# Retention and an MLP in one kernel: the attention work of two chunks joined into larger TensorE groups

## The chip, the cores and the metric

The kernel runs on one core of a Trainium2 chip. The metric is the device time of one execution in microseconds (us). Of the kernel before, five executions took 311.14 to 312.42 us, median 312.0.

A core has five engines that run side by side and meet through semaphores: TensorE (PE: matmuls, with weight loads that overlap them, PEld), VectorE (DVE), ScalarE (ACT), GpSimd (POOL) and SyncE (SP, which here issues DMAs). Each engine takes its instructions in the order in which the code issues them. Matmul results land in PSUM, which has eight banks of 128 x 512 float32; TensorE can only reuse a bank when the engine that empties it is done. TensorE and VectorE or ScalarE work on SBUF otherwise.

## The reference

Inputs are q, k and v (8 batches, 8 heads, 576 positions, 64 dimensions) and two weights (512 x 2048 and 2048 x 512). Per batch and head:

```python
scores = scale * q @ k.T                       # 576 x 576
Dmat   = where(i >= j, gamma_h ** (i - j), 0)  # gamma_h = 1 - 2 ** (-5 - h)
attn   = (scores * Dmat) @ v                   # 576 x 64
```

The heads' results stand side by side as rows of x (4608 x 512), and the output is

```python
h = x @ w_in
g = 0.5 * h * (1 + tanh(c * (h + 0.044715 * h ** 3)))
out = g @ w_out
```

## The kernel before, in words

**Attention in chunks.** The 576 positions of a batch are four chunks of 128 and a tail of 64. The powers of gamma are multiplied into k and q when they are cast to float16 (`cast`, L232), so that within a chunk only a causal mask is left. The steps of a chunk c of batch b are:

- `turn` (L275): TensorE transposes k and q of the chunk (batches 0 to 2 and all tails). From batch 3 on `turn_dma` (L293) does it for a whole batch with two DMA transposes on SP's queue, which wait for the batch's casts.
- `score` (L304): eight matmuls per chunk, of 64 rows each, in pairs that use the upper and lower half of the array (64x128); two PSUM banks. VectorE multiplies each bank by the mask and writes it as float16 into a `ret` tile (L319).
- `state` (L328) and `scan` (L341): eight matmuls of k against v, with 64 columns each (128x64), give the chunk's part of the running state; VectorE adds it to the state so far and decays it (`vs`, `ws`).
- `spread` (L351): ScalarE casts the two halves of the state into a block-diagonal float16 tile (`tbd`; after the last chunk `tbt`, which the tail uses).
- `av` (L356): eight matmuls of `ret` against v (128x64), then, for c > 0, four full matmuls (128x128, L381) that add the product with the state of the chunks before. The tail adds four of 64 columns (L373).
- `put` (L389): ScalarE copies the result out of PSUM into `xT`, the transposed input of the MLP.

A tail holds two groups of four heads one above the other, so it is half as wide. It is loaded, cast and processed some stages after its batch.

**MLP in stages.** Stage t (0 to 8) computes 512 rows: t < 8 the four chunks of batch t, stage 8 all tails. Stages 1 to 8 have 30 steps. Steps 0 to 15 are `up` (L403): four matmuls of 128 x 512 into one of two `hp` banks, and ScalarE's GELU into `gT`; 128 of the inner 2048 per step. Stage 1 uses `up_half` (L419) in these steps. After every fourth step VectorE forms sums and differences of the blocks of `gT` (`act_sums`, L473, four instructions). Steps 16 to 29 are `prod` (L485): seven block products (a Strassen-like scheme with weight sums made once, `weight_sums`, L461), each in two steps of eight matmuls of 256 columns into bank A, B or C, in the order 1, 6, 5, 7, 2, 3, 4. `after` (L505) combines them on VectorE and ScalarE: after product 1 ScalarE copies A, after product 6 (step 19) VectorE adds B (L531), and product 7 (steps 22, 23) goes on adding into the same bank B.

**The order.** All engines' order is written by hand. `at(t, u, f)` (L629) hangs work behind step u of stage t, and works hung on one step run in the order in which they were registered. The sums of a step come after all that hangs on it. Batch b = t + 1 is processed in stage t. `group` (L666) issues one chunk per group: its scores, its state, then the values (`av`) of the group before; `put` a step later and the two spreads two and three steps later. In stages 2 to 6 the groups stand behind steps 6, 11, 16, 21 (chunks 0 to 3) and 26 (the tail of batch t - 2); in stage 1 behind 8, 13, 18 and 23, in stage 7 (the last three tails) behind 2, 7 and 12. Banks of the attention work are t0, t1 and t2 in turn for scores and states, and C or `hp` for values.

From batch 3 on, the casts of batch t + 2 hang on stage t, steps 16 to 23. GpSimd casts k and q, ScalarE v. GpSimd first runs a one-element copy, `gate` (L704), that waits for the last sum of step 15, and loads are held (`q_ld["hold"]`) until `turn_dma` behind step 24 has issued the transposes. Tails are loaded from GpSimd's queue (six DMAs each, L83).

## Time and profile before

| what | value |
|---|---|
| median of 5 executions | 312.0 us |
| the profiled execution | 311.83 us, its span 309.9 us |
| mean granted TensorE clock | 0.996 of full |
| TensorE busy | 297.8 us, 96% of the span |
| VectorE, ScalarE, GpSimd busy | 181.0, 170.3, 121.6 us |
| stage 1 | starts at 55.54, ends at 91.77 us |
| stage 2 | ends at 123.98 us |
| stages 3 to 6 | 31.41 us each, the last ends at 249.63 us |
| stage 7 | ends at 278.82 us |
| the last matmul | starts its row at 304.69, ends at 305.7 us |

The profile comes from one execution. The span runs from its first to its last instruction; what lies outside the span (1.9 us) is the same program's start and end. Lists of instructions give start and length in us, the engine, the line of the kernel, the operation, and the tiles written and read. A matmul's start is recorded, its end is modelled and lies after the start of the next, so distances between starts say more about TensorE than lengths. A list of waits gives who waited for whom, the total, the number and the longest.

### The profile page before, as it was taken

To read this page: it belongs to the slowest core of one execution; us is meant where nothing else is said; L and a number is where in the kernel's file an instruction comes from. 1 tells how busy PE (TensorE), PEld (TensorE's weight loads), DVE (VectorE), ACT (ScalarE), POOL (GpSimd) and SP (SyncE) were. 2 spreads that over 40 slices of the span, in tenths; PEclk is the share of its full clock that TensorE was granted. 3 is DMA by queue.
4 is the path that set the end of the run, shared out by engine and by line. 5 is a ranking of instruction groups with operands and counts; after the bars stand their busy time and mean duration, and the time that the engine had idled before them with its cause. 6 is when DMAs were issued, how large, how long until landed. Compare 5 with 4: busy or idle time off the path is not lost.

```text
span 309.9 us, 6884 instructions
## 1 busy us (share of the span) xinstructions
PE 297.8 (96%) x2779; PEld 199.2 (64%) x2779; DVE 181.0 (58%) x368; ACT 170.3 (55%) x327; POOL 121.6 (39%) x177
## 2 busy tenths in 40 slices
PE   7889999899998999999999999999999999999994
PEld 3458755688884488448844785478547854784583
DVE  6651766789954676476637673776376545522431
ACT  6566417877545763576357745664466346406600
POOL 8669114650871069105910591049651430000000
PEclk9999999999999999999999999999999999999998
DMA  7999999999999995997499849933920040003004
GB/s 204 216 316 376 361 271 225 220 238 244 206 173 183 218 269 116 207 204 221 86 212 212 222 75 180 223 118 69 271 73 19 17 172 0 2 0 135 2 0 135
DMA packets 125983, 51.82 MB, mean 167 GB/s; under 512 B 114176, under 2 KB 116736, under 8 KB 125952
## 3 DMA queue, kind: packets, MB, share of 16 engines
q1 hardware_dynamic: 123936, 47.72, 71.5%
q0 software_dynamic: 1536, 3.15, 4.5%
q10 hardware_dynamic: 480, 0.52, 0.6%
q8 instruction: 21, 0.34, 0.5%
q14 instruction: 10, 0.08, 0.1%
HBM read 36.70 MB, written 9.44 MB: 149 GB/s over the span
## 4 chain that ended last, share of the span: by engine, by line
PE 77%; DMA 6%; SPq 5%; POOL 4%; issue 3%; DVE 2%; ACT 2%; POOLq 0%; DVEq 0%
PE hp L409 30%; PE opB L498 12%; PE opA L498 8%; PE opC L498 8%; PE hp L426 5%; PE op L445 4%; SPq L95 3%; PE st L313 3%; DMA tt<-cq 3%; PE xs L363 2%; DMA ld<-in_moe_w_in_dram 2%; POOL cq L253 2%; PE xs L381 2%; PE us L333 2%; DMA ld<-in_q_dram 2%
## 5 line engine op out<-in xcount | busy, mean ns | idle before, releaser
L409 PE MATMUL hp<-xT,w_in_sb 128*128 128x512 f16 x448 | 101.4, 379 | 0.0
L415 ACT ACTIVATE gT<-hp 128x512 f16<-128x512 f32 x112 | 66.8, 597 | 51.2 <-PE hp L409 50.6
L409 PEld LDWEIGHTS <-w_in_sb 128*128 128x128 f16 x448 | 42.6, 98 | 49.1 <-issue 2.9
L319 DVE TENSOR_TENSOR ret<-st,cm 128x512 f16<-128x512 f32 x64 | 41.1, 684 | 23.6 <-PE st L313 23.5
L498 PEld LDWEIGHTS <-gT 128*128 128x128 f16 x512 | 49.2, 98 | 7.6 <-issue 0.7
L253 POOL TENSOR_TENSOR ck<-ld,sc 128x512 f16<-128x512 f32 x31 | 34.6, 1115 | 22.0 <-DMA ld<-in_k_dram 20.5
L498 PEld LDWEIGHTS <-s 128*128 128x128 f16 x384 | 37.2, 98 | 4.2
L480 DVE TENSOR_TENSOR s<-gT 128x512 f16<-128x512 f16 x32 | 13.6, 426 | 40.8 <-ACT gT L415 39.9
L498 PE MATMUL opA<-w_out_sb,gT 128*128 128x256 f16 x256 | 32.4, 273 | 0.0
L426 PE MATMUL hp<-xT,w_in_sb 128*128 128x256 f16 x256 | 30.1, 273 | 2.3 <-POOL w_in_sb L565 1.0
L498 PE MATMUL opB<-wt,gT 128*128 128x256 f16 x256 | 30.7, 273 | 0.5 <-DVE ost L512 0.5
L426 PEld LDWEIGHTS <-w_in_sb 128*128 128x128 f16 x256 | 24.5, 98 | 6.0 <-issue 1.8
L704 POOL COPY gate<-s 128x1 f16<-128x1 f16 x5 | 0.9, 187 | 68.7 <-DVE s L483 68.7
L253 POOL TENSOR_TENSOR cq<-ld,sc 128x512 f16<-128x512 f32 x24 | 26.1, 1089 | 2.7 <-DMA ld<-in_q_dram 2.7
L399 ACT CAST xT<-xs 128x512 f16<-128x512 f32 x32 | 18.7, 586 | 12.4 <-PE xs L381 11.8
L432 ACT ACTIVATE gT<-hp 128x512 f16<-128x512 f32 x32 | 19.1, 597 | 8.4 <-PE hp L426 8.4
L354 ACT CAST tbd<-ws 64x256 f16<-64x256 f32 x48 | 19.4, 403 | 5.7 <-DVE ws L349 5.1
L240 ACT CAST cv<-ld 128x512 f16<-128x512 f32 x27 | 16.2, 619 | 2.8 <-DMA ld<-in_v_dram 2.5
L512 DVE TENSOR_TENSOR k<-k,opB 128x512 f32<-128x512 f32 x16 | 10.9, 684 | 10.2 <-PE opB L498 10.1
L512 DVE TENSOR_TENSOR ost<-k,opC 128x512 f32<-128x512 f32 x16 | 11.0, 687 | 9.6 <-PE opC L498 9.4
L565 DVE CAST w_out_sb<-ld 128x512 f16<-128x512 f32 x16 | 9.1, 582 | 12.3 <-DMA ld<-in_moe_w_out_dram 12.3
L498 PE MATMUL opC<-w_out_sb,s 128*128 128x256 f16 x128 | 16.1, 273 | 0.0
(97 smaller groups left out, 381.3 us busy)
## 6 DMA issues: line engine op xcount, KB each, us to landing
ld<-in_q_dram SPq DMA_DIRECT2D x32, 256.0 KB, 5.2
ld<-in_k_dram SPq DMA_DIRECT2D x32, 256.0 KB, 5.4
ld<-in_v_dram SPq DMA_DIRECT2D x32, 256.0 KB, 5.1
out_dram<-ost SPq DMA_DIRECT2D x16, 512.0 KB, 4.7
ld<-in_moe_w_in_dram SPq DMA_DIRECT2D x16, 256.0 KB, 5.8
ld<-in_moe_w_out_dram SPq DMA_DIRECT2D x16, 256.0 KB, 6.1
lt<-in_k_dram POOLq DMA_DIRECT2D x16, 64.0 KB, 4.6
lt<-in_q_dram POOLq DMA_DIRECT2D x16, 64.0 KB, 4.5
```

The source lines that it names most:

```text
L240: eng.copy(out=dst, in_=raw)
L253: eng.tensor_tensor(out=dst.rearrange("p (h d) -> p h d", d=D), in0=raw.rearrange("p (h d) -> p h d", d=D), in1=sc[:, s0 : s0 + nh].unsque ...
L319: nc.vector.tensor_tensor(out=r[:, 0:w], in0=st[hl][:, 0:w], in1=m.rearrange("p n i -> p (n i)"), op=ALU.mult)
L354: cp(out=(tbd[b % 2][r, c, :, r] if c < NC - 1 else tbt[b % 4][r, :, r]), in_=att[b]["w"][r])
L399: nc.scalar.copy(out=xT[:, g0 : g0 + 2], in_=src)
L409: nc.tensor.matmul(hp.rearrange("p (g t) -> p g t", t=TL), w_in_sb[:, ct, 128 * fc : 128 * fc + 128], xT[:, o : o + TB // TL, ct, :], star ...
L415: nc.scalar.activation(out=gT[t][:, fc].rearrange("p i n -> p (i n)"), in_=hp, func=AF.Gelu_apprx_tanh)
L426: nc.tensor.matmul(hp[:, 256 * x : 256 * x + 256].rearrange("p (g t) -> p g t", t=TL), w_in_sb[:, ct, 128 * (f + x) : 128 * (f + x) + 128] ...
L432: nc.scalar.activation(out=gT[t][:, f : f + 2, 2 * u : 2 * u + 2, :].rearrange("p f i n -> p f (i n)"), in_=hp.rearrange("p (f n) -> p f n ...
L480: nc.vector.tensor_tensor(out=s["1"], in0=a21, in1=a22, op=ALU.add)
L498: nc.tensor.matmul(op[tag][:, HD * u : HD * u + HD], lhs(f), rhs[:, f], start=(new and u == 0 and f == 0), stop=(f == NH - 1), skip_group_ ...
L512: nc.vector.tensor_tensor(out=o, in0=a, in1=b, op=ALU.add)
```

## The change

From batch 2 on, the attention work is issued in larger groups. In stage t, for batch b = t + 1 and, from stage 3 on, the tail of batch e = t - 3:

- behind step u0: the scores of chunks 0 and 1 and of the tail;
- behind u1: the states of chunks 2 and 3 (both into one bank), the values of chunks 0 and 1 and of the tail, and then all their products with the states (now a function of its own, `inter`);
- behind u2: the scores of chunks 2 and 3;
- behind u3: the states of chunks 0 and 1 of the next batch, and the values and products of chunks 2 and 3.

The four steps are 11, 17, 21, 26 in stage 1, 8, 14, 19, 25 in stage 2, and 6, 12, 17, 24 in stages 3 to 6. A tail's turn moves to step 3 of its stage, its casts from step 15 to 14, and it is processed a stage later. In stage 7 tails 4 and 5, then 6 and 7 go through in pairs. Banks are named by hand: scores also use A, B, C and `hp`. The `ret` tiles become four of full width and two of half width for tails of batches 0 to 4 and 6, in place of five of full width. In stage 1 the casts and the turns of batch 2 move to other steps.

```diff
--- before.py
+++ after.py
@@ -315,9 +315,10 @@
                 )
         m = cm if c < NC else tm
         for hl in range(2):
-            r = sb.tile([128, 512], F16, tag="ret", name="ret", bufs=5)
+            tag, n = ("ret", 4) if c < NC or b in (5, 7) else ("rett", 2)
+            r = sb.tile([128, 512 if tag == "ret" else 256], F16, tag=tag, name=tag, bufs=n)[:, 0:w]
             nc.vector.tensor_tensor(
-                out=r[:, 0:w], in0=st[hl][:, 0:w], in1=m.rearrange("p n i -> p (n i)"), op=ALU.mult
+                out=r, in0=st[hl][:, 0:w], in1=m.rearrange("p n i -> p (n i)"), op=ALU.mult
             )
             a["ret"][c, hl] = r
 
@@ -325,39 +326,38 @@
         c = c % NC
         return slice(512 * c + 128 * p + 64 * hl, 512 * c + 128 * p + 64 * hl + 64)
 
-    def state(b, c, tag="att"):
-        a = att[b]
-        us = bank(tag, "us")
+    def state(b, c, us=None, n=0):
+        a = att[b]
+        us = bank("att", "us") if us is None else us
         for p in range(HP):
             for hl in range(2):
                 nc.tensor.matmul(
-                    us[64 * hl : 64 * hl + 64, 64 * p : 64 * p + 64],
+                    us[64 * hl : 64 * hl + 64, 256 * n + 64 * p : 256 * n + 64 * p + 64],
                     a["k"][:, col(c, p, hl)],
                     a["v"][:, col(c, p, hl)],
                     start=True, stop=True,
                 )
-        a["U"] = us
+        a["U", c] = us[:, 256 * n : 256 * n + 256]
 
     def scan(b, c):
         a = att[b]
-        uc = a.pop("U")[:, 0:256].rearrange("p (q d) -> p q d", d=64)
+        uc = a.pop(("U", c)).rearrange("p (q d) -> p q d", d=64)
         if c > 0:
             s = sb.tile([128, HP, 64], F32, tag="vs", name="vs", bufs=2)
             nc.vector.tensor_tensor(out=s, in0=uc, in1=a["w"], op=ALU.add)
             uc = s
-        a["w"] = w = sb.tile([128, HP, 64], F32, tag="ws", name="ws", bufs=2)
+        a["w"] = a["w", c] = w = sb.tile([128, HP, 64], F32, tag="ws", name="ws", bufs=2)
         nc.vector.tensor_tensor(out=w, in0=uc, in1=gt, op=ALU.mult)
 
     def spread(b, c, cp, hls=(0, 1)):
         for hl in hls:
             r = slice(64 * hl, 64 * hl + 64)
-            cp(out=(tbd[b % 2][r, c, :, r] if c < NC - 1 else tbt[b % 4][r, :, r]), in_=att[b]["w"][r])
+            cp(out=(tbd[b % 2][r, c, :, r] if c < NC - 1 else tbt[b % 4][r, :, r]), in_=att[b]["w", c][r])
 
     def av(b, c, tag="att"):
         a = att[b]
         n = HP if c < NC else 2
-        td = tbd[b % 2]
-        xs = bank(tag, "xs")
+        a["xs", c] = xs = bank(tag, "xs")
         for p in range(n):
             for hl in range(2):
                 nc.tensor.matmul(
@@ -366,6 +366,9 @@
                     a["ret"][c, hl][:, 128 * p : 128 * p + 128],
                     start=(p == 0), stop=True, skip_group_check=True,
                 )
+
+    def inter(b, c):
+        xs = att[b]["xs", c]
         if c == NC:
             for s in range(2):
                 for u in range(2):
@@ -380,14 +383,13 @@
             for p in range(HP):
                 nc.tensor.matmul(
                     xs[:, 128 * p : 128 * p + 128],
-                    td[:, c - 1, p, :],
+                    tbd[b % 2][:, c - 1, p, :],
                     tq(b, c, p),
                     start=False, stop=True, skip_group_check=True,
                 )
-        a["xs"] = xs
 
     def put(b, c):
-        xs = att[b].pop("xs")
+        xs = att[b].pop(("xs", c))
         if c == NC:
             nc.scalar.copy(
                 out=xT[:, GM + b].rearrange("p (u s) t -> p s u t", u=2),
...
@@ -596,7 +597,7 @@
 
     def first(c):
         score(0, c, ST[c % 2])
-        state(0, c, ("A", "t2")[c % 2])
+        state(0, c, bank(("A", "t2")[c % 2], "us"))
         scan(0, c)
 
     first(0)
@@ -615,18 +616,18 @@
             spread(0, c, A.copy)
             filler(3, "C")
         av(0, c, "B")
+        inter(0, c)
         put(0, c)
 
-    PLAN = {1: zip((8, 13, 18, 23, 27), [(2, c) for c in range(NC)] + [()])}
-    for t in range(2, 7):
-        PLAN[t] = zip((6, 11, 16, 21, 26), [(t + 1, c) for c in range(NC)] + [(t - 2, NC)])
-    PLAN[7] = zip((2, 7, 12, 17), [(5, NC), (6, NC), (7, NC), ()])
-    TAILS = {b: ((b + 2, 5), (b + 2, 15)) for b in range(5)}
-    TAILS |= {5: ((6, 16), (6, 24)), 6: ((6, 25), (7, 4)), 7: ((7, 5), (7, 9))}
+
+    TAILS = {5: ((6, 15), (6, 24)), 6: ((6, 25), (7, 8)), 7: ((7, 9), (7, 14))}
+    TAILS |= {b: ((b + 2, 5), (b + 2, 14)) for b in range(5)}
     gate = const.tile([128, 1], F16, name="gate")
     events = {}
 
     def at(t, u, f):
+        if t > 0 and u > 29:
+            t, u = t + 1, u - 30
         events.setdefault((t, u), []).append(f)
 
     def run(t, u):
@@ -653,7 +654,7 @@
     for c in range(NC):
         at(*CU[c], lambda c=c: (cc(1, "k", c, P), cc(1, "v", c, A if c else P)))
         at(*TU[c], lambda c=c: turn(1, c, A.copy))
-        at(*VU[c], lambda c=c: (av(1, c, "AB"[c] if c < 2 else "att"), put(1, c), spread(1, c, A.copy)))
+        at(*VU[c], lambda c=c: (av(1, c, "AB"[c] if c < 2 else "att"), inter(1, c), put(1, c), spread(1, c, A.copy)))
     for c in range(NC):
         at(*SU[c], lambda c=c: (score(1, c), state(1, c), scan(1, c)))
     at(1, 9, lambda: weight_sums(4, "32"))
@@ -661,41 +662,68 @@
     at(1, 20, lambda: weight_sums(4, "4"))
 
 
-    late = []
-
-    def group(t, u, b=None, c=0):
-        prev = late.pop() if late else None
-        if b is not None:
-            if b < NPE or c == NC:
-                at(t, u - 2, lambda: turn(b, c, V.tensor_copy))
-            at(t, u, lambda: score(b, c))
-            if c < NC:
-                at(t, u, lambda: (state(b, c), scan(b, c)))
-                at(t, u + 2, lambda: spread(b, c, A.copy, (0,)))
-                at(t, u + 3, lambda: spread(b, c, A.copy, (1,)))
-            late.append((b, c))
-        if prev:
-            at(t, u, lambda: av(*prev, "C" if u < NF else "hp"))
-            at(t, u + 1, lambda: put(*prev))
-
-    def tail_in(t, u, b):
-        at(t, u, lambda: load_tail(b))
-
-    def tail_cast(t, u, b):
-        at(t, u, lambda: (new_tail(b), [cc(b, key, NC, e) for key, e in zip("kqv", (P, P, A))]))
+    def scores(t, u, *xs):
+        at(t, u, lambda: [score(*x) for x in xs])
+
+    def states(t, u, b, c, tag):
+        def go():
+            us = bank(tag, "us")
+            for n in range(2):
+                state(b, c + n, us, n)
+            for n in range(2):
+                scan(b, c + n)
+        at(t, u, go)
+        def sp(n, hl):
+            at(t, u + 2 + 2 * n + hl, lambda: spread(b, c + n, A.copy, (hl,)))
+        for n in range(2):
+            for hl in range(2):
+                sp(n, hl)
+
+    def values(t, u, *xs):
+        at(t, u, lambda: ([av(*x) for x in xs], [inter(*x[:2]) for x in xs]))
+        for n, x in enumerate(xs):
+            at(t, u + 1 + n, lambda x=x: put(*x[:2]))
+
+    def turn_tail(b, k):
+        t, u = (b + 3, 3) if b < 4 else (7, 1 if b < 6 else 15)
+        at(t, u, lambda: turn(b, NC, V.tensor_copy, "t2" if b % 2 else "t0"))
+
+    def turns_of(t, u, b, c, tag):
+        at(t, u, lambda: turn(b, c, V.tensor_copy, tag))
 
     for b, (l, k) in TAILS.items():
-        tail_in(*l, b)
-        tail_cast(*k, b)
-    for t, us in PLAN.items():
-        for u, x in us:
-            group(t, u, *x)
+        at(*l, lambda b=b: load_tail(b))
+        at(*k, lambda b=b: (new_tail(b), [cc(b, key, NC, e) for key, e in zip("kqv", (P, P, A))]))
+        turn_tail(b, k)
+
+    for t in range(1, 7):
+        b, e = t + 1, t - 3
+        if t == 1:
+            for c, (u, tag) in enumerate(((7, "t2"), (9, "A"), (15, "C"), (18, "hp"))):
+                turns_of(t, u, b, c, tag)
+            u0, u1, u2, u3 = 11, 17, 21, 26
+            states(t, u0, b, 0, "B")
+            scores(t, u0, (b, 0, ("t0", "t1")), (b, 1, ("t2", "A")))
+        else:
+            u0, u1, u2, u3 = (8, 14, 19, 25) if t == 2 else (6, 12, 17, 24)
+            tail = [(e, NC, ("B", "C"))] if e >= 0 else []
+            scores(t, u0, (b, 0, ("t0", "t1")), (b, 1, ("t2", "A" if t > 2 else "C")), *tail)
+        states(t, u1, b, 2, "t0")
+        values(t, u1, (b, 0, "t1"), (b, 1, "t2"), *([(e, NC, "B")] if e >= 0 else []))
+        scores(t, u2, (b, 2, ("t1", "t2")), (b, 3, ("hp", "hp")))
+        if t < 6:
+            states(t, u3, b + 1, 0, "t0")
+        values(t, u3, (b, 2, "t1"), (b, 3, "t2"))
+    for n, u in enumerate((3, 17)):
+        x, y = (4 + 2 * n, NC), (5 + 2 * n, NC)
+        scores(7, u, x + (("t0", "t1"),), y + (("hp", "hp") if n else ("t2", "A"),))
+        values(7, u + 4, x + ("t2" if n else "B",), y + ("t0" if n else "C",))
 
     for b in range(2, B):
         ent = [(key, c) for c in range(NC) for key in "kqv"]
         eng = {"k": P, "q": P, "v": A}
         if b == 2:
-            t0, ut = 1, [1, 1, 2, 6, 6, 7, 11, 11, 12, 16, 16, 17]
+            t0, ut = 1, [1, 1, 2, 4, 4, 5, 9, 9, 10, 13, 13, 14]
         else:
             t0, ut = b - 2, [16, 16, 17, 18, 18, 19, 20, 20, 21, 22, 22, 23]
         at(t0, ut[0], lambda b=b: (new_casts(b), new_turned(b)))
```

More of the change, by code (lines that the diff above doesn't have):

```diff
@@ L571 @@
     }
-    CH = range(NC + 1)
     def cc(b, key, c, eng):
```

## The prediction

> **What bounds the kernel now.** Times are us from the span's start; "t:u" is step u of stage t. I read the page's busy shares and clock first, then TensorE's waits, then the order of instructions on TensorE, ScalarE, VectorE and the two queues around one attention group.
>
> ```profile
> PE 297.8 (96%) x2779; PEld 199.2 (64%) x2779; DVE 181.0 (58%) x368; ACT 170.3 (55%) x327; POOL 121.6 (39%) x177
> PEclk9999999999999999999999999999999999999998
> ```
> TensorE is never off for long and its clock is full. Its waits for other engines say the same: apart from the start, one DMA wait and crumbs.
>
> ```profile
> PE fill L213 <- POOL wide L180: 2.3, 1, 2.3
> PE st L313 <- DMA tt<-cq: 1.0, 1, 1.0
> PE opB L498 <- DVE ost L512: 0.5, 1, 0.5
> ```
> So TensorE's own sequence is the time. TensorE in order of time, around group 4:11:
>
> ```profile
> 166.53 0.38 PE L409 MATMUL hp<-xT,w_in_sb 128*128 128x512 f16 x1
> 166.84 0.40 PE L313 MATMUL st<-tt 64*128 64x128 f16 x8
> 167.17 0.32 PE L333 MATMUL us<-cv,ck 128*64 128x64 f16 x8
> 167.32 0.39 PE L363 MATMUL xs<-ret,cv 128*64 128x128 f16 x8
> 167.65 3.72 PE L409 MATMUL hp<-xT,w_in_sb 128*128 128x512 f16 x16
> ```
> Starts show what the modelled ends hide. Matmuls of 512 columns follow each other every 0.216, yet the scores start 0.31 after the last one: 0.095 lost where the array goes from 128x128 to 64x128. A lone pair of score matmuls follows the one before in 0.056, but the states come 0.146 after the last score pair: 0.09 lost from 64x128 to 128x64. From 128x64 back to 128x128 it is 0.152 instead of 0.056: 0.096. States to values (both 128x64) lose nothing. No semaphore separates these rows, so I call the 0.095 the price of a change of form.
>
> **What the change removes.** Before, each group has three such changes (a last group two). Counted in the order of the code: stage 1 14, stages 2 to 6 15 each, stage 7 11: 100. After: a group of scores has two, a group of states, values and inter-chunk products two: stage 1 9, stages 2 to 7 8 each: 57. 43 x 0.095 = 4.1. Nothing in the trace goes straight from 64x128 to 128x128, which the change now does 14 times; its bounds are 0 and 0.096, and I take 0.095, since the three kinds seen lie within 0.006; at 0 it would be 1.3 faster. Longer groups also save first pairs (0.011 a score group, 0.02 a state group, 0.02 at the old tail's): 0.12 a stage.
>
> Weighed against the Trainium skill: TensorE: Matmul & The Clock Gate, Single matmul latency, gives a lone warm matmul (398+N)/2.4 ns, 166 ns over its streaming; a full drain at that price would make the 43 changes worth an estimated 7.1 us. The 0.095 of the rows decides.
>
> Stage by stage, TensorE's bare work is 64 up matmuls x 0.2156 + 112 products x 0.1092 = 26.03. Attention in stages 3 to 6 before: groups 0.911 + 0.897 + 1.130 + 1.131 + 0.893 and the tail's turn 0.223 = 5.185, and 0.20 of small waits: 31.41, the period of the trace (155.39 to 186.81). After, with rows 0.056 a pair (0.032 for states), 0.234 an inter-chunk product, 0.126 a tail's: u0 0.755, u1 1.387, u2 0.643, u3 1.386, turn 0.223 = 4.394.
>
> **What the change makes wait, stages 3 to 6.** The evictions come in bursts, in the order of the code, on queues that keep it. ScalarE before, from 4:12 on:
>
> ```profile
> 168.72 0.60 ACT L415 ACTIVATE gT<-hp 128x512 f16<-128x512 f32 x1 [1.17 <-PE hp L409]
> 169.21 0.58 ACT L399 CAST xT<-xs 128x512 f16<-128x512 f32 x1
> 169.68 0.62 ACT L415 ACTIVATE gT<-hp 128x512 f16<-128x512 f32 x1
> 170.32 0.41 ACT L354 CAST tbd<-ws 64x256 f16<-64x256 f32 x1
> ...
> 171.66 0.60 ACT L415 ACTIVATE gT<-hp 128x512 f16<-128x512 f32 x1
> 172.28 0.41 ACT L240 CAST ev<-lt 128x256 f16<-128x256 f32 x1
> ```
> Put step 12's first matmul at 0. GELU starts 1.07 after its step's start and ends 0.60 later; here GELU 15 ended at 4.62. After: up 12 takes 0.863, group u1 1.387, so step 13 starts at 2.25, 14 at 3.11, 15 at 3.98, the product of step 16 at 4.84. ScalarE: GELU 13 3.32, put of chunk 0 3.81, GELU 14 4.28 to 4.90, tail cast to 5.32, spread to 5.75, put of chunk 1 5.66 (some start 0.1 before the one ahead ends, as in the rows above), GELU 15 6.12 to 6.74: 1.1 later than TensorE alone would have it. Then spread to 7.16 and the tail's put to 7.55.
>
> VectorE before:
>
> ```profile
> 172.29 0.42 DVE L480 TENSOR_TENSOR s<-gT 128x512 f16<-128x512 f16 x1 [1.47 <-ACT gT L415]
> ...
> 173.43 0.42 DVE L483 TENSOR_TENSOR s<-gT,s 128x512 f16<-128x512 f16 x1
> 173.76 1.28 DVE L319 TENSOR_TENSOR ret<-st,cm 128x512 f16<-128x512 f32 x2
> ...
> 176.36 0.68 DVE L512 TENSOR_TENSOR k<-k,opB 128x512 f32<-128x512 f32 x1
> ```
> The four sums wait for GELU 15 and take 1.59. After: 4 evictions of scores (2 before, each 0.60 to the next) at u2=17 stand ahead of the add of step 19, which so ends at 6.74 + 1.49 + 2.42 + 0.68 = 11.33. TensorE would start step 22, which overwrites what the add reads, at 4.84 + 6 x 0.873 + 0.643 = 10.72. The stall is 0.65. (Product 18 waits 0.37 of it for bank B, held by the tail's put.) Bounds: 0, if ScalarE's pile is only the 0.6 that TensorE leaves it, and 1.25, if GpSimd's casts stretch the add by the 0.6 by which they stretched a scan (0.43 to 1.03, just ahead of the last row). I take 0.65. Two of the three small waits of a stage (0.15) go with the spreads that move. Period: 26.03 + 4.394 + 0.044 + 0.65 = 31.12, gain 0.29 in each of stages 3 to 5; stage 6 issues no states (0.276): 0.57. Sum 1.44.
>
> **DMA transposes.** GpSimd's gate waits for the last sum of step 15, its 8 casts follow, then SP's two transposes, then the next stage's first scores.
>
> ```profile
> 173.98 0.19 POOL L704 COPY gate<-s 128x1 f16<-128x1 f16 x1 [15.62 <-DVE s L483]
> ...
> 181.50 1.04 POOL L253 TENSOR_TENSOR cq<-ld,sc 128x512 f16<-128x512 f32 x1
> ```
> and on SP's queue:
>
> ```profile
> 183.50 4.98 SPq L296 DMA_TRANSPOSE tt<-cq  x1
> ```
> The trace's completion marks put the landing 20.67 after the gate for stage 1's, then 17.43, 17.42, 18.49, 17.44. The scores came 19.01 after it. After, the gate is at 6.74 + 1.59 + 0.13 = 8.46 from step 12, and the scores at 26.1 (steps 12 to 15 3.45, u1 1.39, 14 products 12.23, u2 0.64, u3 1.39, 7 up steps 6.04, turn 0.22, form 0.1, the stall 0.65): 17.65, spare 0.2. One landing in four as long as 18.49 would cost 0.9; I take 0.5 (bounds 0 and 3.6). Behind them on SP stand the next batch's loads and the stores of steps 27 and 29; the gate's 15.62 of idle time is what the loads have to spare.
>
> **Stage 2** lost 1.03 to the transpose (98.98 in place of 97.95). Its first scores move from step 6 to 8, 1.73 later. Attention 0.643 + 1.152 + 0.643 + 1.386 = 3.824; stage 1's last spreads fall into ScalarE's steps 0 and 1: 0.29. So 26.03 + 3.82 + 0.04 + 0.29 = 30.19 against 32.21: 2.02.
>
> **Stage 1.** At 1:9 two weight sums (0.68 + 0.69) now stand ahead of the copy of turn 1 (0.68) which the scores of step 11 need; then VectorE has 3 scans, 4 evictions, sums, a copy and sums without a break. From its copy at 66.7 that is 12.0 to 12.9 of work to the end of step 15's sums, 78.7 to 79.4 (78.2 before); then a weight sum 1.28, four scans 2.5, the copy of turn 3 0.68, to 83.1 to 83.8, where TensorE wants it at 82.6 to 83.3; the add behind it delays step 22 again. Step 22 starts at 83.8 to 84.5, 8 products (6.99) and u3 (1.39) remain: 92.2 to 92.9 against 91.77. I take a loss of 0.8; bounds 0.3 and 1.6. Transposes then land at 99.5 to 100.2, scores wait for nothing at 100.4 to 101.1. Batch 2's casts come earlier in GpSimd's queue, but there wait for loads as before; v3's cast passes the gate's hold, so one more load (1.1 of SP's issue) goes ahead of the transposes, in SP's idle time.
>
> **Stage 7**: 0.446 + 0.423 + 0.68, twice, = 3.10 against 3.14; at step 8 a tail cast (0.41) and a put (0.37) meet between GELUs, and the step after next waits 0.46. Loss 0.45. Tail loads (6 issues x 0.62 on GpSimd's queue) and casts there run ahead of TensorE: the last tail was cast at 250.9 and is turned at 262, so the moved places cost nothing. The other tails' ScalarE cast, a step earlier, is in the pile above. The smaller ret tiles cost nothing: their readers are done one group earlier.
>
> **Sum**: 1.44 - 0.5 + 2.02 - 0.8 - 0.45 = 1.7. The profiled execution took 311.83 (span 309.9 and 1.9 around it): 310.1. The median is 0.2 above it: 310.3.
>
> A rule that speaks against the change: TensorEngine Tiling (Array Packing), PSUM Bottleneck, says packing speeds TensorE and not the emptying of PSUM, which may become the limit. That is what the 0.65 is; the page gives no price.
>
> **Rivals.** (a) The queues keep up: no 0.65, 0.5, 0.8 or 0.75 of stages 2 and 7: 310.3 - 4.6 = 305.7. For it: VectorE and ScalarE are under 60% busy. Against: both orders above. 12%. (b) The waits eat it: with 1.25 for 0.65 in four stages and 1.6 for 0.8 in stage 1, 310.3 + 2.4 + 0.8 = 313.5; at half of that 311.9, no change. For it: both queues run without a break where it counts; against: each upper end needs every op stretched. 22%. (c) Slower: the transpose is late in stages 3 to 6. At 19.0 after the gate, between 18.49 and 20.67, three stages lose 1.35 and stage 3, whose scores stand 18.1 after the gate, 0.9: 4.95 where I have 0.5, so 314.8. It ends slower than before from 18.3 on. For it: of five landings one was longer than 19.0 and one 18.49; against: three lie within 0.02 of 17.43. 20%. That the forms don't merge is excluded: TensorE keeps the order of the code.
>
> **How the numbers follow.** Forecast 46%, 307.5 to 311.5 on its own. With (a) 12, (b) 22, (c) 20. Two in ten left out, half of (a) and the far end of (c): 306.8 to 313.8. A measurement of this kernel tells 0.3% (0.94) from none: faster = forecast and (a), 0.58; same = most of (b) and the mild end of (c), 0.2; slower the rest, 0.22.
>
> **What would show it.** Score starts 0.31 after an up matmul and 57 changes of form; stage 4 at 31.1; GELU 15 ending 6.7 after step 12; TensorE waiting for L512 at step 22; no DMA wait in stage 2. Wrong if scores wait for tt, or if stage 1 ends after 94.

## The result: 0.4% faster, and the profile after

The kernel after took 309.76 us (median of 44 executions, 307.97 to 311.98), the kernel before 310.95 beside it on the same chips (79 executions, 309.24 to 314.23). The ratio is 0.996, with a 95% interval of 0.9949 to 0.9971. The prediction was 310.3 against a median of 312.0, a ratio of 0.9946, so the direction and the range were right and the gain was forecast a little too large.

The profiled execution of after took 311.14 us, its span 308.3 (2.8 outside the span, where before had 1.9). The span is 1.6 shorter than that of before; the prediction's sum was 1.7. First the busy shares and the clock from the page of after:

```profile
PE 294.1 (95%) x2779; PEld 199.4 (65%) x2779; DVE 179.9 (58%) x368; ACT 168.5 (55%) x327; POOL 120.7 (39%) x177
PEclk9999999999999999999999999999999999999999
```

TensorE is busy for 3.7 us less with the same 2779 matmuls and still decides the time, but its share fell: part of what it saved became waiting. TensorE's waits of after (total, number, longest):

```profile
PE fill L213 <- POOL wide L180: 2.3, 1, 2.3
...
PE st L313 <- DMA tt<-cq: 1.0, 1, 1.0
PE opC L500 <- DVE ost L514: 1.0, 1, 1.0
PE st L313 <- DVE tt L288: 0.9, 1, 0.9
...
PE opB L500 <- ACT xT L394: 0.6, 4, 0.2
```

The first line was there before. The DMA wait has the same size as before but another place: it stood in stage 2 and is now in stage 5. The other three are not in the list of the profiled execution of before. The opC and tt lines are in stage 1; the opB line is one short wait in each of stages 3 to 6. One stage, then, between the first matmul of one stage and that of the next, in us:

| stage | before | after | gain | gain predicted |
|---|---|---|---|---|
| 1 | 36.23 | 37.27 | -1.04 | -0.8 |
| 2 | 32.21 | 30.16 | 2.05 | 2.02 |
| 3 | 31.41 | 31.15 | 0.26 | 0.29 |
| 4 | 31.41 | 30.97 | 0.44 | 0.29 |
| 5 | 31.41 | 32.07 | -0.66 | 0.29 |
| 6 | 31.41 | 30.72 | 0.69 | 0.57 |
| 7 | 29.19 | 29.35 | -0.16 | -0.45 |
| transposes late, one of stages 3 to 6 | | (in stage 5) | | -0.5 |
| sum | | | 1.58 | 1.71 |

Around group 4:12 TensorE's rows of after are:

```profile
166.46 0.44 PE L334 MATMUL us<-cv,ck 128*64 128x64 f16 x16
166.73 0.62 PE L363 MATMUL xs<-ret,cv 128*64 128x128 f16 x16
167.18 0.28 PE L363 MATMUL xs<-rett,ev 128*64 128x128 f16 x4
167.39 0.40 PE L384 MATMUL xs<-tt,tbd 128*128 128x128 f16 x4
...
172.18 0.62 PE L313 MATMUL st<-tt 64*128 64x128 f16 x16
172.95 1.91 PE L500 MATMUL opB<-wt,s 128*128 128x256 f16 x16 [0.15 <-ACT xT L394]
174.69 1.91 PE L500 MATMUL opC<-wt,s 128*128 128x256 f16 x16
176.72 1.91 PE L500 MATMUL opB<-wt,gT 128*128 128x256 f16 x16
```

The groups did merge: 16 states and 20 value matmuls in a row with no change of form between them. Two starts are late. The opB row after the scores has its wait printed beside it. The last row starts 2.03 after the opC row, where sixteen such matmuls take 1.75: 0.28 of waiting that the trace does not name. What stands behind both is in the rows of ScalarE (first fence) and VectorE (second) in the same stage:

```profile
170.41 0.40 ACT L240 CAST ev<-lt 128x256 f16<-128x256 f32 x1
170.72 0.40 ACT L355 CAST tbd<-ws 64x256 f16<-64x256 f32 x1
171.03 0.57 ACT L401 CAST xT<-xs 128x512 f16<-128x512 f32 x1
171.50 0.59 ACT L417 ACTIVATE gT<-hp 128x512 f16<-128x512 f32 x1
...
172.53 0.37 ACT L394 CAST xT<-xs 128x256 f16<-128x256 f32 x1
```

```profile
172.12 0.43 DVE L482 TENSOR_TENSOR s<-gT 128x512 f16<-128x512 f16 x1 [2.52 <-ACT gT L417]
...
173.59 2.48 DVE L320 TENSOR_TENSOR ret<-st,cm 128x512 f16<-128x512 f32 x4
175.99 0.68 DVE L514 TENSOR_TENSOR k<-k,opB 128x512 f32<-128x512 f32 x1
```

ScalarE runs a tail cast, a spread and a put without a gap ahead of GELU 15 (171.50). VectorE stands idle for 2.52 until that GELU has written `gT`, then does four sums, four evictions of scores and only then the add (L514). The opB row at 176.72 overwrites the bank that this add reads, and starts when the add is done (176.67).

### The profile page after: what moved, and what is told of

Its sections match the earlier page's. It is cut to its first block, busy times and chain, and to the rows that moved or that the text cites. A ratio compares the mean times of both kernels' runs of the same rounds, so it can differ in the third digit from the quotient of the medians.

```text
span 308.3 us, 6895 instructions
## 1 busy us (share of the span) xinstructions
PE 294.1 (95%) x2779; PEld 199.4 (65%) x2779; DVE 179.9 (58%) x368; ACT 168.5 (55%) x327; POOL 120.7 (39%) x177
## 4 chain that ended last, share of the span: by engine, by line
PE 64%; DVE 15%; SPq 5%; ACT 5%; DMA 5%; POOL 3%; issue 2%; DVEq 0%; POOLq 0%
PE hp L411 28%; PE opB L500 9%; PE opC L500 6%; PE hp L428 5%; PE opA L500 5%; DVE ret L320 4%; PE op L447 3%; SPq L95 3%; DMA tt<-cq 3%; DVE wt L471 2%; ACT gT L417 2%; PE xs L363 2%; DMA ld<-in_moe_w_in_dram 2%; PE st L313 2%; PE xs L384 2%
## 5 line engine op out<-in xcount | busy, mean ns | idle before, releaser
L320 DVE TENSOR_TENSOR ret<-st,cm 128x512 f16<-128x512 f32 x64 | 40.0, 682 | 10.9 <-PE st L313 10.9
L500 PE MATMUL opA<-w_out_sb,gT 128*128 128x256 f16 x256 | 31.2, 273 | 0.0
L544 ACT COPY ost<-opA 128x512 f32<-128x512 f32 x8 | 4.7, 584 | 37.0 <-PE opA L500 29.4
L514 DVE TENSOR_TENSOR k<-k,opB 128x512 f32<-128x512 f32 x16 | 10.9, 682 | 18.5 <-PE opB L500 18.5
L401 ACT CAST xT<-xs 128x512 f16<-128x512 f32 x32 | 18.5, 583 | 4.0 <-PE xs L384 3.5
L514 DVE TENSOR_TENSOR ost<-k,opC 128x512 f32<-128x512 f32 x16 | 11.0, 687 | 13.1 <-PE opC L500 12.8
L500 PE MATMUL opC<-w_out_sb,s 128*128 128x256 f16 x128 | 15.4, 272 | 1.0 <-DVE ost L514 1.0
```

What stands on the lines that cost most here:

```text
L320: nc.vector.tensor_tensor(out=r, in0=st[hl][:, 0:w], in1=m.rearrange("p n i -> p (n i)"), op=ALU.mult)
L401: nc.scalar.copy(out=xT[:, g0 : g0 + 2], in_=src)
L500: nc.tensor.matmul(op[tag][:, HD * u : HD * u + HD], lhs(f), rhs[:, f], start=(new and u == 0 and f == 0), stop=(f == NH - 1), skip_group_ ...
L514: nc.vector.tensor_tensor(out=o, in0=a, in1=b, op=ALU.add)
```

## The experiments

Two theories were put against each other. The first is the prediction's: a change of form on TensorE costs 0.095, and what the merged groups save is partly given back as waits in fixed places, each behind one named queue. The rival has two branches: the gain comes from something else in the change (a later place for the first group), or the waits are one pool that merely moves when a part of it is removed. "Before" below is always the kernel before on the same chip, and each run's ratio is against it.

### The kernel after again, and its scores and values split

> The changed kernel as it is, the base for the other runs. Theory (fewer changes of form, part of it given back as waits): 0.996 of the time before; stage 4 lasts 30.97 us, TensorE loses 0.22 before product 18 and 0.28 before product step 22 in each of stages 3 to 6, 1.05 at the scores of 1:11, 1.16 before 1:26, and waits up to 1.1 for the DMA transpose in one stage. Rival (the wait for the transpose belongs to one place in the order and not to chance): it falls into stage 5 again.

Measured: 309.19 against 310.99, ratio 0.9948 (0.9916 to 0.998). Stages 1 to 7 were 37.39, 30.17, 31.34, 30.98, 31.51, 30.72 and 29.35. Stages 2, 4, 6 and 7 repeat to 0.01; 1, 3 and 5 do not, which the sections on stage 1 and on the transposes take up. A third execution of after that was profiled, in the run again2, had 38.13, 30.16, 31.15, 30.97, 30.97, 30.71 and 29.35.

The split keeps every tile and bank, and takes back 18 changes of form:

```diff
-            scores(t, u0, (b, 0, ...), (b, 1, ...), *tail)
+            scores(t, u0, (b, 0, ...))
+            scores(t, u0 + 1, (b, 1, ...), *tail)
...
-        values(t, u3, (b, 2, "t1"), (b, 3, "t2"))
+        values(t, u3 + (1 < t < 6), (b, 2, "t1"), (b, 3, "t2"))
```

> Scores of chunk 1 (and the tail) one step after those of chunk 0 in stages 2 to 6, and the values of chunks 2 and 3 one step after the states in stages 2 to 5: 18 more changes of the array's form, the same matmuls. Theory (a change of form costs TensorE 0.095 us): 18 x 0.095 = 1.7 us more than the changed kernel, and with the longer first pairs 1.8. Rival (the forms cost nothing that other work would not fill, and the gain came from the transpose's wait in stage 2): within 0.4 us of the changed kernel.

Measured: 311.27, ratio 0.9994 (0.9971 to 1.0016), 2.08 above the unsplit kernel on the same chip. Stage 2 was 30.61 (+0.44), stage 4 31.41 (+0.43), stage 6 30.93 (+0.21): four, four and two changes, or 0.11 for each with the first pair of a group that comes with it. Stages 3 and 5 were 31.62 and 31.41, 0.47 and 0.44 above the executions of after that wait for no transpose there; the five stages add up to 1.99. TensorE's rows of the split kernel at its first two groups of stage 4:

```profile
161.64 0.40 PE L313 MATMUL st<-tt 64*128 64x128 f16 x8
161.97 1.04 PE L411 MATMUL hp<-xT,w_in_sb 128*128 128x512 f16 x4
162.94 0.40 PE L313 MATMUL st<-tt 64*128 64x128 f16 x8
```

From the first score to the next up matmul it is 0.33: the first pair at 0.067, two more at 0.056, and 0.148 from the last pair's start to the up matmul, which is 0.092 more than a pair that follows its own kind. This is the direction (64x128 to 128x128) that the trace of before did not show. The theory of the changes of form holds in both kind and size: 18 of the 43 changes put back, which cost about as much as the whole net gain.

### How much of the gain is the later place

The first group of stage 2 stood behind step 6 and waited 1.0 for the transposes. Here only that is changed in the kernel before:

```diff
-        PLAN[t] = zip((6, 11, 16, 21, 26), ...)
+        PLAN[t] = zip((6, 11, 16, 21, 26) if t > 2 else (8, 12, 16, 21, 26), ...)
```

> The kernel before, with stage 2's first two groups behind steps 8 and 12 in place of 6 and 11, as late as the changed kernel's. Theory: the wait of 1.0 us for the DMA transpose at 98.98 goes and nothing takes its place: 1.0 us less than before, ratio 0.997, so most of the net gain of the change could be had without larger groups. Rival: the wait is only passed on to the next transposes, whose gate hangs on the same stage: no change.

> The kernel before with stage 2's first two groups behind steps 8 and 12, on the same chip. Theory: 0.997 of the time before, no wait for a transpose in stage 2; the changed kernel, whose larger groups save 0.44 in each of stages 3 to 6 and lose 1.0 in stage 1, is 0.1 to 0.3% faster than this.

> The changed kernel as it is, on the same chip as the runs beside it. Theory: 0.995 to 0.996 of the time before, stage 4 at 30.97, a wait of 1.17 before 1:26.

Measured: 310.23, ratio 0.9962 (0.9936 to 0.9988), and on a second chip 310.58, ratio 0.9971 (0.9944 to 0.9998). The kernel after stood beside them at 309.19 and, the second time, 309.42 (ratio 0.9948, 0.992 to 0.9977). TensorE's rows of the first of these two runs at the start of stage 2:

```profile
91.36 7.97 PE L409 MATMUL hp<-xT,w_in_sb 128*128 128x512 f16 x36
99.26 0.40 PE L313 MATMUL st<-tt 64*128 64x128 f16 x8
```

The scores follow the up matmuls with no wait, and stage 2 is 31.04 in place of 32.21, 1.17 less where 1.0 was expected. So 0.76 of the median (0.41 the second time) comes from a change of two numbers, and the merged groups themselves are worth about 1.0 to 1.2 on top of that, in this kernel as it is planned. Medians of 11 or 12 executions leave that difference uncertain, but the stages agree: from stage 1 to 7, after was 1.15 and 1.39 shorter than this kernel in the two pairs of profiled executions. So the rival's first branch is true in part; the prediction had counted the two together in stage 2's 2.02.

### The two waits of stages 3 to 6

If the short wait ahead of product 18 and the one ahead of step 22 hang on one queue, removing the first only enlarges the second. The tail's values go to bank C, so that product 18 need not wait for the tail's put:

```diff
-        values(t, u1, ..., *([(e, NC, "B")] if e >= 0 else []))
+        values(t, u1, ..., *([(e, NC, "C")] if e >= 0 else []))
```

> The changed kernel with the tail's values in bank C in place of B, so that product 18 need not wait for the tail's put. Theory (VectorE's queue, four evictions ahead of the add of step 19, sets when step 22 can start): the 0.22 before product 18 goes and the wait before step 22 grows from 0.28 to 0.50; time as the changed kernel's within 0.2 us. Rival (the two waits are separate): 4 x 0.22 = 0.9 us less.

Measured: 310.05, ratio 0.9973 (0.9943 to 1.0003); stage 4 30.97, exactly as without the edit. The median is 0.86 above that of after on the same chip, where at most 0.2 was expected; the intervals overlap, stages 3, 4 and 6 are those of after to 0.01, and the profiled execution lost 1.36 in stage 5 to a late transpose, which this edit does not touch. Its TensorE rows there:

```profile
171.71 0.62 PE L313 MATMUL st<-tt 64*128 64x128 f16 x16
172.26 1.92 PE L500 MATMUL opB<-wt,s 128*128 128x256 f16 x16
174.02 1.91 PE L500 MATMUL opC<-wt,s 128*128 128x256 f16 x16
176.26 1.91 PE L500 MATMUL opB<-wt,gT 128*128 128x256 f16 x16 [0.33 <-DVE k L514]
```

The wait after the scores is gone, and the one before the last row has grown to 0.33 (0.49 by starts) and now carries its releaser's name: VectorE's add. The two were one wait, set by VectorE's queue behind GELU 15. Next, GELU 15 itself is brought forward: the put of chunk 1 goes behind it, and ScalarE's cast of the tail's v to step 18, for the tails of batches 0 to 3.

```diff
-            at(t, u + 1 + n, lambda x=x: put(*x[:2]))
+            at(t, u + 1 + n + (n > 0 and u == 12), lambda x=x: put(*x[:2]))
...
-        at(*k, lambda b=b: (new_tail(b), [cc(b, key, NC, e) for key, e in zip("kqv", (P, P, A))]))
+        at(*k, lambda b=b: (new_tail(b), [cc(b, key, NC, P) for key in "kq"]))
+        at(k[0], 18 if b < 4 else k[1], lambda b=b: cc(b, "v", NC, A))
```

The tail's values stay in bank C.

> The changed kernel with less on ScalarE between GELU 14 and GELU 15 in stages 3 to 6: the tail's v cast behind step 18 (stages 3 to 5 only, stage 2 too), the put of chunk 1 behind step 15 and the tail's behind 16, and the tail's values in bank C. Theory (ScalarE's pile delays GELU 15, and with it sums, evictions and the add that step 22 waits for): GELU 15 ends 0.5 to 0.8 earlier, both waits (0.22 and 0.28) go, 0.5 a stage, 2.0 us less than the changed kernel; the gate comes earlier too and stage 5's wait for the transpose (0.5 to 1.3) shrinks. Rival (VectorE's four evictions alone make the wait, whenever GELU 15 ends): no change.

Measured: 308.69 against 310.56, ratio 0.9943 (0.9921 to 0.9965). Stages 3 to 5 were 30.86, 30.67 and 30.67: 0.30 less than after in stages 3 and 4, where 0.5 was expected. GELU 15 ended 17.20 after the start of stage 4, where it ended at 17.98 in after, so the rival (the evictions alone make the wait) is out. Both waits are gone in these stages, and a smaller new one has come (first fence TensorE, second the moved put on ScalarE):

```profile
171.05 1.91 PE L500 MATMUL opA<-w_out_sb,gT 128*128 128x256 f16 x16
172.89 0.81 PE L313 MATMUL st<-tt 64*128 64x128 f16 x16
173.63 1.92 PE L500 MATMUL opB<-wt,s 128*128 128x256 f16 x16
```

```profile
172.46 0.59 ACT L401 CAST xT<-xs 128x512 f16<-128x512 f32 x1
```

The 16 score matmuls take 0.74 to the next row, where without a wait they take 0.55 (the rows of the joined kernel below): in the middle of them TensorE waits for bank t2, which the put that was moved now empties later (173.05). Stage 6 gained nothing (30.72): its tail's v cast was left in place, and TensorE waits 0.50 among the scores there. The stage says what the median of this run could not say by itself (on other chips after had the same ratio).

### Stage 1

Two weight sums on VectorE were suspected, each ahead of something TensorE needs. Each was moved alone: `32` from 1:9 to 1:12, and `4` from 1:20 to 1:24.

```diff
-    at(1, 9, lambda: weight_sums(4, "32"))
+    at(1, 12, lambda: weight_sums(4, "32"))
```

> The changed kernel with the two weight sums behind 1:9 moved behind 1:12, so that the copy which the scores of 1:11 wait for stands ahead of them. Theory (VectorE works without a break from 63 to 88, and stage 1 is as long as its queue): the wait of 0.4 to 1.2 at 1:11 goes and the one before 1:26 grows by as much; stage 1 stays at 37.4 within 0.3. Rival (the order alone costs): 0.5 to 1 us less.

```diff
-    at(1, 20, lambda: weight_sums(4, "4"))
+    at(1, 24, lambda: weight_sums(4, "4"))
```

> The changed kernel with the weight sum behind 1:20 (1.33 us on VectorE, needed at 1:28) moved behind 1:24, past the four evictions and two adds that bank C waits for. Theory (VectorE's queue sets the end of stage 1): the wait before 1:26 (1.16) goes, stage 1 1.1 us shorter. Rival (stage 1 is set by the casts and loads): no change.

VectorE's and TensorE's rows of after around the second of the two waits (first fence VectorE):

```profile
82.83 1.33 DVE L471 TENSOR_TENSOR wt<-w_out_sb,wt 128x1024 f16<-128x1024 f16 x1
84.08 2.47 DVE L320 TENSOR_TENSOR ret<-st,cm 128x512 f16<-128x512 f32 x4
86.48 0.67 DVE L514 TENSOR_TENSOR k<-k,opB 128x512 f32<-128x512 f32 x1
87.19 0.69 DVE L514 TENSOR_TENSOR ost<-k,opC 128x512 f32<-128x512 f32 x1
```

```profile
85.02 1.91 PE L500 MATMUL opA<-w_out_sb,gT 128*128 128x256 f16 x16
87.93 1.03 PE L500 MATMUL opC<-w_out_sb,s 128*128 128x256 f16 x8 [1.00 <-DVE ost L514]
```

TensorE at step 26 wants bank C, which VectorE reads last in a row of seven instructions that begins with the weight sum (the four evictions are one line). With that sum moved, the same row of TensorE in that kernel is

```profile
87.01 1.03 PE L500 MATMUL opC<-w_out_sb,s 128*128 128x256 f16 x8
```

with 0.06 of waiting by modelled ends, 0.23 by starts (1.17 in after). It took 308.76 against 310.56, ratio 0.9943 (0.9922 to 0.9964). The median alone doesn't show the gain, since after had about the same ratio on other chips; the trace does. From the first product of step 16 to the end of stage 1 it is 16.08, where the three profiled executions of after have 17.01 to 17.02: the wait is removed, and nothing took its place there. The whole stage was 37.20, against 37.27, 37.39 and 38.13, and not the 1.1 less that was expected, largely because the wait at 1:11, which this edit leaves alone, was 1.13 in this execution.

Moving `32` did the opposite: 309.99, ratio 0.9985 (0.9966 to 1.0003), no gain over after. In its trace the wait at 1:11 is gone and TensorE waits later instead:

```profile
85.95 0.40 PE L313 MATMUL st<-tt 64*128 64x128 f16 x8 [0.49 <-DVE tt L288]
86.54 1.91 PE L500 MATMUL opB<-wt,gT 128*128 128x256 f16 x16 [0.19 <-DVE k L514]
...
91.50 1.03 PE L500 MATMUL opC<-w_out_sb,s 128*128 128x256 f16 x8 [1.31 <-DVE ost L514]
```

VectorE runs from 61 to 88 us of after with no gap over 0.11, and work that goes one place later there is late for the next reader. From step 16 to the end stage 1 took 18.39, 1.37 more than in after; steps 10 to 15 took 6.71, 0.5 to 1.05 less. It had been expected that the two would balance within 0.3; from step 10 on this execution is 0.3 to 0.9 longer. Its first steps can't be compared: it was the slowest of its twelve (312.99), and the granted clock of TensorE was 0.5 to 0.7 in each microsecond from 58 to 62, where eight matmuls took 1.86 in place of 1.03.

### The transposes

The landing of the transposes, counted from the gate, was 20.68, 18.07, 16.74, 18.64 and 16.22 in after. Only stage 5 waits for one. TensorE's and SP's rows there:

```profile
188.80 2.75 PE L411 MATMUL hp<-xT,w_in_sb 128*128 128x512 f16 x12
192.59 0.62 PE L313 MATMUL st<-tt 64*128 64x128 f16 x16 [1.04 <-DMA tt<-cq]
```

```profile
184.27 3.30 SPq L296 DMA_TRANSPOSE tt<-cq  x1
```

Over the executions that were profiled this wait was 1.10 (by starts), 0.54 and 0.0 in the kernel after, without any edit. In the second of them the scores of stage 3 also waited, 0.18.

The place in the order matters, as the rival in the run again had it. In the eleven profiled executions of after and of kernels made from it, the transposes issued in stage 2 landed 17.9 to 18.5 after the gate, those of stage 3 16.55 to 16.94, those of stage 5 16.2 to 17.2, and those of stage 4, for which stage 5 waits, 16.8 to 18.9. In all of these stages GpSimd's casts ended 8.2 after the gate and the first transpose was issued 7.2 after it, so the difference arises later. Every wait over 0.2 fell in stage 5, in six of the eleven executions, with a size that varies. A first group behind step 7 leaves 0.86 more:

```diff
-            u0, u1, u2, u3 = (8, 14, 19, 25) if t == 2 else (6, 12, 17, 24)
+            u0, u1, u2, u3 = (8, 14, 19, 25) if t == 2 else (7, 12, 17, 24)
```

> The changed kernel with the first scores of stages 3 to 6 behind step 7 in place of 6. Theory (the scores are the first to need the DMA transposes, which land 16.2 to 18.7 us after the gate, 17.5 after it in the changed kernel): the wait in stage 5 (0.5 to 1.3) falls by 0.86 or goes, other stages unchanged: 0.4 to 0.9 us less. Rival (the later evictions push VectorE's sums and with them the gate): no change or slower.

Measured: 309.4, ratio 0.996 (0.9934 to 0.9985), with a wait of 0.38 in stage 5. That is inconclusive: the ratio is that of after itself, and the landing of the transposes issued in stage 4 varies by 2.1 between executions, more than the 0.86 that the edit moves. What sets the landing time of a DMA transpose stays open.

### All of it together

The edits that removed a wait or were meant to (bank C, the lighter ScalarE queue, `4` at 1:24, the first group behind step 7) were joined. One line was added against the new wait for bank t2: the spreads around the moved put are ordered so that it goes first.

```diff
-            at(t, u + 2 + 2 * n + hl, lambda: spread(...))
+            at(t, u + 2 + 2 * n + hl + (u == 12 and n < hl), lambda: spread(...))
```

> The changed kernel with the shorter ScalarE queue (tail's v cast, puts and the second spread of chunk 2 after GELU 15, tail's values in bank C), the last weight sum behind 1:24, and the first scores of stages 3 to 6 behind step 7. Theory (each wait has its own cause and they add up): stages 3 to 5 at 30.5 each against 30.97, 0.47 x 3 = 1.4; stage 1 shorter by 1.0; stage 5's wait for the transpose (0.5 to 1.3) gone; 3.0 us less than the changed kernel, about 306.5. Rival (a wait that goes is replaced by the next): 1 us less at most.

Measured: 306.72 against 310.99, ratio 0.9843 (0.9807 to 0.9879); after on this chip had 309.42, so the gain over it is 2.70 where 3.0 was expected (six executions of joined, 305.27 to 307.61). Stages 3 to 6 were 30.67, 30.49, 30.49 and 30.23. Stage 4 of it on TensorE:

```profile
171.21 0.62 PE L313 MATMUL st<-tt 64*128 64x128 f16 x16
171.76 1.92 PE L500 MATMUL opB<-wt,s 128*128 128x256 f16 x16
173.52 1.91 PE L500 MATMUL opC<-wt,s 128*128 128x256 f16 x16
175.27 1.91 PE L500 MATMUL opB<-wt,gT 128*128 128x256 f16 x16
```

Starts now follow at 0.55, 1.76 and 1.75: nothing is left to wait for. The rival's second branch, a pool of waits that only moves, holds for the bank C edit and for `32` alone and is refuted here. This is the prediction's rival (a), the queues keeping up, brought about by hand. It named 305.7, 6.3 below the median of before that it started from; joined is 4.27 below its own. Rival (a) also counted the losses of stage 7 and of all of stage 1 as gone, which are still there in part.

The last run moved the sums `32` to GpSimd, behind step 15, on top of this:

```diff
-            nc.vector.tensor_tensor(out=wt[o][:, s], in0=x[:, s], in1=y[:, s], op=f)
+            eng.tensor_tensor(out=wt[o][:, s], in0=x[:, s], in1=y[:, s], op=f)
...
-    at(1, 9, lambda: weight_sums(4, "32"))
+    at(1, 15, lambda: weight_sums(4, "32", P))
```

> The same, and the two weight sums of 1:9 on GpSimd behind 1:15 (it has nothing to do from 70 to 78) in place of VectorE. Theory (stage 1 is as long as VectorE's queue): VectorE has 1.4 to 2.1 less ahead of the scores of 1:11, their wait (0.4 to 1.3) goes: 0.4 to 1.3 us less than without this. Rival (GpSimd's sums slow VectorE's beside them, as its casts stretch them from 0.42 to 1.27): no change or slower.

Measured: 307.46, ratio 0.9867 (0.982 to 0.9914), no better than joined, and in the profiled execution, the slowest of six (309.13, the others 305.06 to 308.80), stage 1 is 39.69 in place of 37.17. GpSimd's and then VectorE's rows:

```profile
69.05 2.30 POOL L471 TENSOR_TENSOR wt<-w_out_sb 128x1024 f16<-128x1024 f16 x1
71.43 2.18 POOL L471 TENSOR_TENSOR wt<-wt,w_out_sb 128x1024 f16<-128x1024 f16 x1
```

```profile
69.29 2.34 DVE L484 TENSOR_TENSOR gT<-gT 128x512 f16<-128x512 f16 x1
71.56 2.33 DVE L485 TENSOR_TENSOR s<-gT,s 128x512 f16<-128x512 f16 x1
73.82 0.68 DVE L288 COPY tt<-tr 128x1024 f16<-128x1024 f16 x1
```

Nothing holds these sums back to step 15: GpSimd ran them as soon as it came to them, at 69, where VectorE had the sums and the copy for 1:11 to do. They took GpSimd 2.30 and 2.18 us (VectorE 0.68 when undisturbed). VectorE's own two sums beside them took 2.3 in place of 0.42, the copy of a turn stood behind these, and TensorE waited 2.81 at 1:11 where it waits 0.29 in joined.

## Why the prediction was right, step by step

**The price of a change of form: right.** After shows 0.092 for the direction that was bounded by 0 and 0.096 and taken at 0.095, and the split kernel priced 18 changes at 2.08. The Trainium skill (TensorEngine Tiling (Array Packing), Key Properties) says that a change of tiling mode drains TensorE; these rows show a loss at every such change and give the price that the page lacks; that a drain is what takes the time they do not show.

**Stages 3 to 6, the stall of 0.65: mechanism right, size a little high.** In stage 4 the two waits are 0.22 and 0.28 by starts, 0.50 in all. GELU 15 ended 6.60 after step 12's start where 6.74 was worked out, the add at 11.18 where it was 11.33. That makes stage 4 30.97 in place of 31.12. (The prediction's own two times, 11.33 and 10.72, leave 0.61 between them and not 0.65.) Stage 3 came out at 31.15, but partly by luck: it has the smaller stall and 0.18 that was not foreseen, a spread of stage 2 that falls between its first two GELUs (124.70 to 125.10) and delays its step 3. The path was the one described: shifting the bank only moved the wait (the tail in bank C), and an earlier GELU 15 removed it. The upper end of 1.25 rested on GpSimd's casts stretching the add as they stretched a scan. No such stretch exists for it: the add ran beside a cast and took 0.68, and the last section says why.

**The transposes, 0.5: in the bounds of 0 to 3.6, in this execution too small.** The scores of stage 5 would have come 17.68 after the gate (17.65 was worked out) and the landing came at 18.64 (one landing of 18.49 had been foreseen). The first group waited 1.10 there and in no other stage. Three executions of the same kernel had 1.10, 0.54 and 0 in stage 5, so the 0.5 is about the mean of what varies. Rival (c), late in all four stages, did not happen.

**Stage 2: right.** 30.16 against 30.19; the scores come at 100.94, 1.6 after the landing. What the step did not separate is that over half of it, 1.17 of 2.05, was a matter of place alone.

**Stage 1, a loss of 0.8: this step failed in its places.** Step 22 and the scores behind 1:21 were to wait for VectorE's copy of turn 3 and add. In after neither waits. TensorE waits for VectorE behind 1:11, for the copy of turn 1 (0.87), and at step 26, for the add that frees bank C (1.00). The late copy of turn 1 was named, but no wait at 1:11 was priced; the one at step 26 was not named. The prediction followed VectorE's queue to step 22 and stopped there, though the weight sum of 1:20, four evictions and two adds stood behind it and bank C was wanted two products on. The size came out nearly right, which is luck as the waits were others: 1.04, and 1.16 in the execution of after whose first steps match those of before to 0.01. The third had a stage 1 of 38.13, 1.18 more than the kernel before in an execution with first steps like its own (36.95, in before_late2). The wait at 1:11 ranged from 0.16 to 1.21 by profile rows in the kernels that left its cause alone; it was 0.16 to 0.29 in the three that reached step 10 latest after the start of the stage, and 0.42 to 1.21, in no order, in the six others.

**Stage 7, a loss of 0.45: mechanism right, size too high.** It lost 0.16. The trace of after has the wait where the prediction put it: a tail cast (257.90) and a put (258.19) stand ahead of GELU 9, which ends at 259.07, and step 11 starts at 259.12, 0.19 late in place of 0.46. No run was made on it.

**The sum.** Measured gain less forecast gain was -0.24 in stage 1, +0.15 and +0.12 in stages 4 and 6, +0.29 in stage 7, and -0.45 in stage 5 with its transposes (0.66 lost where 0.21 net was worked out). These almost cancel, 1.58 against 1.71, so that the sum came this close is partly luck. Of the 6.3 that rival (a) counts (1.7 and the 4.6 of losses it leaves out; 1.0 of it is the old wait of stage 2), 1.58 were left in this execution, so waits decide this change as much as forms do; the joined kernel, 4.27 by medians, shows that most of them need not be there.

**The signs.** Scores start 0.31 after an up matmul and stage 4 is 30.97. In stages 1 to 7 the trace has 65 changes of form where before has 108: 43 fewer, as counted (the count of 57 and 100 leaves out eight of batch 1's, which both kernels have). The add is named at step 22 only in the trace of the bank C edit, and stage 2 waits for no DMA. One of the two signs of being wrong did appear: scores wait for `tt`, in stage 5. The sum had set 0.5 aside for just this, so the two parts of the prediction do not fit together. Stage 1 ended at 92.79, before 94.

## What to carry to other kernels

Count the changes between tile forms on TensorE and price them from the trace: merging groups removes them, but it also turns an even flow of evictions into bursts, and these are paid for at the next bank reuse. So follow each queue beyond the first late reader until it runs idle, and then reorder what stands ahead of the instruction that releases TensorE: in this kernel a handful of such edits after the merge gave 2.7 us where the merge with its new places had given 1.6. Move the work in front of a wait only to a place where its engine is idle, since on a queue without a break a move makes the next reader late.

## What the runs showed of the hardware

A VectorE instruction with both operands in SBUF that begins while a GpSimd cast or sum runs ends a fixed time after it: it waits until the GpSimd instruction has ended. From 50 us on, after has eleven VectorE instructions that took over 0.15 longer than the shortest of the same line and operands; ten of 128 x 512 or 128 x 256 ended 0.28 to 0.30 after a GpSimd instruction did, the one of 128 x 1024 0.55 after. (One of the ten began 0.12 ahead of its cast, the others after theirs.) An instruction that begins well ahead of the cast keeps its time: the weight sum at 68.70 took 0.69, though a cast began 0.43 into it. In the last run the two sums of 2.34 and 2.33 ended at 71.63 and 73.89, 0.28 after GpSimd's at 71.35 and 73.61. Instructions with an operand in PSUM (evictions, adds, the first half of a scan) never did: all adds of L514 on 128 x 512 took 0.67 to 0.69, and no eviction of L320 was longer than 0.69, beside casts or not. The Trainium skill (SBUF — State Buffer, Who interferes with whom) states such a rule: an instruction of VectorE with two SBUF inputs and a GpSimd instruction that reads SBUF share a port that one of them holds for its whole length. The rows agree, and the prediction could have excluded its stretched add by it.

The landing of a DMA transpose of one batch came between 16.2 and 18.9 us after the gate in stages 2 to 5 of after and the kernels made from it (17.8 to 20.7 in stage 1, where the casts also ended later, 8.95 to 9.4 after the gate). The stage of issue accounts for much of that, but in stage 4 alone it varied by 2.1 between executions; no run here shows what sets it.
